# A recurrent attention with a mixture of experts: the first unit's chain of small products reordered, with banks, spare products, gates and weight loads moved

## The chip, the cores and the metric

The kernel runs on one core of a Trainium2 chip. The metric is the device time of one execution in microseconds. TensorE (PE) makes matrix products into PSUM banks, VectorE (DVE), ScalarE (ACT) and GpSimd (POOL) work on tiles, and SyncE (SP) issues nearly all transfers. Each engine takes its own instructions in a fixed order.

## What is computed

For each of 4 x 8 batch and head pairs a 40 x 40 state runs through 768 steps; its outputs, 3072 tokens of 320 values, go through four experts whose outputs are summed with normalised weights. All is float32.

```python
for t in range(S):                      # B=4, H=8, S=768, D=40
    y[:, :, t] = np.einsum('bhd,bhde->bhe', rt, state)
    Sa = np.einsum('bhde,bhe->bhd', state, at)
    state_decay = state * wt[:, :, None, :] - np.einsum('bhd,bhe->bhde', Sa, bt)
    state = state_decay + np.einsum('bhd,bhe->bhde', vt, kt)
...
p = domain_probs / (domain_probs.sum(-1, keepdims=True) + 1e-09)
for e in range(E):                      # E=4, F=1024
    h = np.maximum(x @ w1[e], 0.0)
    out += p[:, e:e + 1] * (h @ w2[e])
```

## The kernel before

The sequence is cut into 12 chunks of 64 steps. A *unit* is one chunk of two batches (16 heads), so there are 24 units; units 0 and 1 are chunk 0. The recurrence inside a chunk becomes products of 64 x 64 matrices and one triangular solve, and only the state passes from chunk to chunk. The mixture takes 128 tokens for units 0 and 1 each and 256 tokens (a whole chunk) from then on; it is most of the work of TensorE.

A unit goes through generators, which a main program written out by hand advances piece by piece with `run(generator, n)`:

- `within(q)` (from L385). Stage 1: the decays are transposed and multiplied up by a scan into G (L398, L402), with `gl` (L400, L406). Stage 2: G is turned on TensorE (pg, L336), and `gp` is made from it with a reciprocal (L414, L415). Stage 3: `n_tok` and `k_tok` (L434, L438), AT (L440, L442). Stage 4: both are turned (pNT, pKT) and copied by ACT to NT and KT (L420). Then come the score products pfe, 32 of which are for F and 32 for ET, into the same two banks (L482 to L488; two instructions of the trace for each product); ACT copies F (L491), DVE copies the upper part to ET (L494). The V and R inputs of units 0 to 2 are turned on TensorE (L450: half plain transposes, half products with the identity that swap halves, one ACT copy each to RT and VT), later units' by DVE. RT and VT make the products pc, masked by DVE into VC (L431). ET and V make pev, copied to EV (L505).
- `substitute(q, eng)` (L513) solves the triangular systems. Four pieces of F are copied to `blocks` (L518: two by ACT, two by DVE), transposed to M (L521), a first pair of columns is taken up (L528 to L537), and 16 pairs of steps fill Z (L544, L554 or L557). DVE does units 0 and 1, GpSimd the others.
- `merge(q)` (L563) transposes Z to Qc and QTc (L568, L570), makes pY and pQ (L583, L595) and puts QT together.
- `step(q)` (L603): psat and pst (L631, L637), copied to SaT and SX; pxr (L651), masked into SX (L660); pdy (L674), from which Y and the new state come (L682 to L693); pxT (L699), copied to xT (L703), the input of the mixture.
- `mixture_of_unit` (L762): for each expert eight blocks of hidden columns in two halves (x0 and x1), `ups` (ph, L726 and L734), and `down` (po, L775), whose result DVE scales and adds to osb (L750, L752). `normalize` (L301) turns the gates (pp, L306) and divides them by their sum on DVE (L307 to L315).

PSUM has two sets of banks: five of the tag `big` for all small products, and three of the tag `mm` for ph and po. The weights of the first layer come in *pieces* of 640 KB (`load_piece`, L263; half an expert), those of the second in 1280 KB for one expert (`load_w2`, L298). The order of instructions on each engine is worked out when the program is built; `keep_in_program_order` (called `pin` in `within`) keeps an instruction where the program has it. `keep_warm(n)` (L931) issues n spare products of the identity (32 and 72 instructions in the trace for n = 16 and 36).

The main program starts at L937: unit 0 goes alone up to its solve on DVE (L950), 36 spare products stand behind pg of unit 1 (L960), then unit 0's merge and step, and from L976 the mixture of unit 0 with units 1 and 2 between. From L1002 a loop over the units does the rest.

Of the kernel before, what the change touches and what calls it, by code (L numbers as in the profile page):

```python
# [7 lines left out]
FP32 = mybir.dt.float32  # L8
# [7 lines left out]
def kernel(  # L16
# [55 lines left out]
    def big(name):  # L72
        return ps.tile([P, 512], FP32, name=name, tag="big", bufs=5)
# [227 lines left out]
    def normalize():  # L301
        n = B // 2 * NC
        pp = big("pp")
        flat = probs.rearrange("p i t e -> p (i t) e")
        for e in range(E):
            nc.tensor.transpose(out=pp[:, e * n:(e + 1) * n], in_=flat[:, :, e], identity=ident[0:n, 0:n])  # L306
        ins = nc.vector.tensor_copy(  # L307
            out=gate[:], in_=pp[:, 0:E * n].rearrange("p (e b c) -> p c b e", b=B // 2, c=NC),
        )
        tc.keep_in_program_order(ins)  # L310
        nc.vector.reduce_sum(out=total[:], in_=gate[:], axis=AX.X)
        nc.vector.tensor_scalar_add(out=total[:], in0=total[:], scalar1=1e-9)
        nc.vector.reciprocal(out=total[:], in_=total[:])
        nc.vector.tensor_mul(gate[:], gate[:], total[:, :, :, None].to_broadcast([P, NC, B // 2, E]))
        nc.vector.tensor_scalar_mul(out=minus_gate[:], in0=gate[:], scalar1=-1.0)  # L315

    def half(s):
# [23 lines left out]
    def tok(x):  # L341
        return lambda j: x[:, 2 * j:2 * j + 2, :].rearrange("p h e -> p (h e)")
# [42 lines left out]
    def within(q):  # L385
# [3 lines left out]
        def pin(ins, also=False):  # L389
            if q.u < PADDED or also:  # L390
                tc.keep_in_program_order(ins)
# [7 lines left out]
        q.gl = sb.tile([P, 2 * NJ, 1], FP32, name="gl", tag="gl", bufs=4)  # L399
        pin(nc.vector.tensor_copy(out=q.gl[:, :, 0], in_=G[:, L::L]))  # L400
        pin(nc.vector.memset(Gv[:, :, 0:1], 0.0))
# [12 lines left out]
        pin(nc.vector.tensor_tensor(out=gp[:], in0=pg, in1=n["W"][:], op=ALU.mult))  # L414
        pin(nc.vector.reciprocal(out=gp[:], in_=gp[:]))  # L415
        yield

# [7 lines left out]

        def causal_scores():
            pc = quadrants(banks("pc"), 0, BY_TOKENS, L, lambda j, s, i: (
                d_half(j, s), i, j, of_slots(VT, d_half(j, s), j, i, D), of_slots(q.RT, d_half(j, s), j, i, D),
            ))
            for r in range(2):  # L430
                pin(causal(of_d_half(q.VC[:, :, D:D + L], r), pc[r]), q.start)  # L431
# [13 lines left out]
        if q.u > 0:  # L445
            nc.scalar.copy(out=q.VC[:, :, 0:D], in_=token_V())
        VT = sb.tile([P, 2 * NJ, L], FP32, name="VT", tag="turned", bufs=3)
        q.RT = sb.tile([P, 2 * NJ, L], FP32, name="RT", tag="RT", bufs=2)

        def turn_padded():  # L450
            for x, t in (("R", q.RT), ("V", VT)):
                p, src = big(f"p{x}T"), n["padded" + x]
                for j in range(NJ):
                    cols = slice(j * P, (j + 1) * P)
                    if j % 2 == 0:
                        nc.tensor.transpose(out=p[:, cols], in_=tok(src)(j), identity=ident[:])
                    else:
                        for s in range(2):
                            nc.tensor.matmul(
                                out=p[half(1 - s), cols], lhsT=src[:, head(j, s), :], rhs=ident[:], start=True, stop=True,  # L460
                            )
                nc.scalar.copy(
                    out=t[:].rearrange("p (i j) t -> p j i t", i=2),
                    in_=p[:].rearrange("p (j i t) -> p j i t", i=2, t=L),
                )

        if q.u >= PADDED:
            turn_raw(VT[:], n["rawV"][:])
            turn_raw(q.RT[:], n["rawR"][:])
        yield  # L470
# [5 lines left out]
        if q.u > 0:  # L476
            if q.u < PADDED:
                turn_padded()
            causal_scores()
            yield  # L480
# [3 lines left out]
            s, i ^ s, j, of_slots(q.AT, s, j, i), of_pairs(NT, s, j, i),  # L484
        ))
        pe = quadrants(p, NJ * L, BY_TOKENS, L, lambda j, s, i: (
            s, i, j, of_pairs(KT, s, j, i), of_slots(q.AT, s, j, i),
        ))  # L488
        q.F = sb.tile([P, H, L], FP32, name="F", tag="F", bufs=2)
        for s in range(2):  # L490
            nc.scalar.copy(out=of_slot(q.F[:], s), in_=pf[s])  # L491
        ET = ETs()
        for s in range(2):
            causal(of_slot(ET[:], s), pe[s])  # L494
        yield
# [12 lines left out]
        if q.u == 0:  # L508
            turn_padded()
            causal_scores()  # L510
        yield

    def substitute(q, eng):  # L513

# [6 lines left out]
        ins = nc.vector.transpose(out=M[:], in_=cols)  # L521
        if q.u == 1 or eng is nc.vector:
            tc.keep_in_program_order(ins)


        pairs = M[:].rearrange("p (c two) r -> p c two r", two=2)
        on_diag = M[:].rearrange("p c r -> p (c r)")[:, Q + 1::2 * (Q + 1)]
        nc.vector.memset(on_diag, 0.0)  # L528

# [3 lines left out]
        below = M[:].rearrange("p c r -> p (c r)")[:, 1::2 * (Q + 1)]  # L533
        nc.vector.tensor_tensor(
            out=by_second, in0=pairs[:, :, 1, :], in1=below[:, :, None].to_broadcast([P, Q // 2, Q]), op=ALU.mult,
        )
        nc.vector.tensor_tensor(out=pairs[:, :, 0, :], in0=pairs[:, :, 0, :], in1=by_second, op=ALU.add)  # L537
        at_once = eng is nc.vector
# [375 lines left out]

    def run(gen, n=99):
        for _ in range(n):
            if next(gen, gen) is gen:
                break
# [17 lines left out]

    ws = [within(units[u]) for u in range(3)]  # L937
    keep_warm(16)
    run(ws[0], 1)
    go(load_raw(units[1], "W"))  # L940
    run(ws[0], 2)
    run(ws[1], 1)
# [6 lines left out]
    run(ws[0], 2)  # L949
    substitute(units[0], nc.vector)  # L950
    run(ws[0], 1)
# [5 lines left out]
    for x in "VR":  # L957
        load_padded(units[2], x)
    run(ws[1], 1)
    keep_warm(36)  # L960
    run(ws[1], 1)
    run(m)
    run(ws[2], 1)
    for e in range(2):
        load_piece()
        load_piece()
        load_w2(e)
    load(units[2], "BK")
    go(load_raw(units[2], "A"))
    go(load_raw(begin(3), "W"))  # L970
    load_piece()
    run(s, 4)
    run(ws[1], 1)
    run(s)
    run(ws[1], 2)
    mixture_of_unit(units[0])  # L976
    substitute(units[1], nc.vector)
    normalize()
    run(ws[1])
# [3 lines left out]
    mix(1)  # L983
    run(ws[2], 2)
    load(units[3], "WBKV")
    go(load_raw(units[3], "AVR"))
    run(m)
    mix(1)
    run(ws[2], 2)
    run(s, 2)  # L990
    run(ws[2], 1)
    substitute(units[2], nc.gpsimd)
    ws.append(within(units[3]))
# [8 lines left out]
    for u in range(1, NU):  # L1002
# [50 lines left out]
        if u + 2 < NU:  # L1053
            substitute(units[u + 2], nc.gpsimd)
        if u + 3 < NU:
            ws.append(within(units[u + 3]))
            run(ws[u + 3], 1)
# [41 lines left out]
```

## Time and profile before

| | |
|---|---|
| median of 7 runs | 1148.47 us (1143.71 to 1153.02) |
| profiled execution | 1147.09 us, of it span 1145.3 us |
| PE busy | 1111.2 us (97%), 16088 products |
| DVE, ACT, POOL busy | 756.7, 335.1, 471.6 us |
| mean granted clock of TensorE | 0.979 |
| transfers | 122.17 MB, mean 107 GB/s |
| ph (L726, L734) | 2280 products, 454.6 us busy |
| products for osb (L841, L775) | 27% and 3% of the chain that ended last |

A row of the timeline has start, duration, engine, line, operation, the tile written and the tiles read, shapes, and a count if several alike are merged; in brackets stand the idle time of the engine before it and what ended it. The chain of waits follows what released each step, back from the last instruction; "issue" in it is time in which an engine waited for nothing that the profile shows. A stretch has the busy time of each engine, then TensorE's granted clock (1.00 is full), the DMA share and GB/s. A busy TensorE can be one at a low clock: its busy time says nothing of its pace.

The mixture's first product starts at 52.58 us and po of expert 0 at 61.27. The solve of unit 0 takes DVE from 22.34 to 32.99 us, that of unit 1 from 60.72 to 71.39. GpSimd starts on unit 2's at 103.34, on unit 3's at 131.64 and on unit 4's at 174.22.

### The profile page before, as it was taken

The numbers are of one execution on the slowest core, as the hardware profiler recorded it, in microseconds if no ns is written. First come the engines' busy times: TensorE is split into PE (matmuls) and PEld (weight loads), VectorE is DVE, ScalarE is ACT, GpSimd is POOL, SyncE is SP. The second block draws the span as 40 slices with busy tenths as digits, with TensorE's granted clock in tenths as the row PEclk, the third lists the DMA queues.
The fourth block names the chain that finished last, engine by engine and source line by source line (L and its number), as shares of the span: only waits on it lengthen the run. The fifth ranks groups of instructions, "written<-read, shape, count | busy, mean of one in ns | idle before, by whom it ended". The sixth has DMA issues, their size and how long they took to land.

```text
span 1145.3 us, 38306 instructions
## 1 busy us (share of the span) xinstructions
PE 1111.2 (97%) x16088; PEld 984.0 (86%) x16088; DVE 756.7 (66%) x1554; ACT 335.1 (29%) x847; POOL 471.6 (41%) x1221
## 2 busy tenths in 40 slices
PE   6899997999999999999999999999999999999998
PEld 5778876888989898888998989989899898888887
DVE  7673657797766867767677677677586686553333
ACT  2222423332342332332332332332322323311110
POOL 4003637644625526526427437346346346340000
PEclk7888999999999999999999999999999999999999
DMA  7874543345353553644543543543444442231320
GB/s 117 235 212 120 107 106 76 91 105 123 79 124 90 125 121 80 139 105 97 129 106 80 143 100 85 134 106 89 117 108 103 117 108 65 76 89 53 104 93 12
DMA packets 268867, 122.17 MB, mean 107 GB/s; under 512 B 213736, under 2 KB 242072, under 8 KB 268696
## 3 DMA queue, kind: packets, MB, share of 16 engines
q1 hardware_dynamic: 265416, 119.12, 42.3%
q8 instruction: 127, 2.08, 0.8%
q10 hardware_dynamic: 3280, 0.61, 0.3%
q14 instruction: 44, 0.36, 0.1%
HBM read 111.79 MB, written 3.93 MB: 101 GB/s over the span
## 4 chain that ended last, share of the span: by engine, by line
PE 85%; DVE 6%; POOL 3%; issue 2%; SPq 1%; DMA 1%; ACT 1%; DVEq 0%; POOLq 0%; ACTq 0%
PE ph L734 29%; PE p L841 27%; PE ph L726 9%; PE pdy L372 3%; PE po L775 3%; POOL Z L557 2%; PE pfe L372 2%; PE psat L372 2%; PE pxr L372 2%; PE prn L372 1%; POOL Z L544 1%; PE pc L372 1%; PE pQ L595 1%; PE pev L372 1%; PE pY L583 1%
## 5 line engine op out<-in xcount | busy, mean ns | idle before, releaser
L734 PE MATMUL ph<-xT,w1p 128*128 128x256 f32 (+1 forms) x1520 | 345.1, 380 | 0.4 <-issue 0.4
L734 PEld LDWEIGHTS ph<-xT,w1p 128*128 128x128 f32 x1520 | 275.2, 191 | 63.2 <-issue 25.3
L544 POOL TENSOR_TENSOR Z<-M,Z 128x62 f32<-128x62 f32 (+7 forms) x352 | 142.2, 404 | 374.8 <-DVE M L537 341.9
L557 POOL TENSOR_TENSOR Z<-Z 128x31 f32<-128x31 f32 (+7 forms) x704 | 256.6, 364 | 55.2
L835 DVE TENSOR_TENSOR a<-hs 128x512 f32<-128x512 f32 x220 | 152.4, 710 | 125.1 <-ACT hs L739 125.1
L739 ACT ACTIVATE hs<-ph 128x512 f32<-128x512 f32 (+1 forms) x208 | 116.0, 564 | 299.5 <-PE ph L734 298.8
L841 PE MATMUL p<-sums,a 128*128 128x160 f32 x1056 | 165.1, 299 | 0.0
L752 DVE SCALAR_TENSOR_TENSOR osb<-p,gate,osb 128x320 f32<-128x320 f32 (+1 forms) x243 | 107.9, 481 | 74.5 <-PE p L841 70.8
L841 PEld LDWEIGHTS p<-sums,a 128*128 128x128 f32 x1056 | 152.9, 190 | 2.3
L726 PE MATMUL ph<-xT,w1p 64*128 64x256 f32 (+1 forms) x760 | 109.5, 399 | 1.8 <-issue 1.7
L841 PE MATMUL p<-w,hs 128*128 128x160 f32 x704 | 102.9, 299 | 0.0
L841 PE MATMUL p<-w,a 128*128 128x160 f32 x704 | 102.8, 299 | 0.0
L841 PEld LDWEIGHTS p<-w,hs 128*128 128x128 f32 x704 | 100.3, 190 | 2.2
L576 POOL COPY QT<-QTc 32x256 f32<-32x256 f32 x96 | 51.4, 535 | 113.5 <-DVE QTc L570 102.9
L841 PEld LDWEIGHTS p<-w,a 128*128 128x128 f32 x704 | 98.0, 190 | 0.0
L726 PEld LDWEIGHTS ph<-xT,w1p 64*128 64x128 f32 x760 | 67.2, 188 | 15.3 <-issue 5.7
L521 DVE STREAM_TRANSPOSE M<-blocks 128x1024 f32<-128x1024 f32 x24 | 47.1, 1962 | 24.9 <-ACT blocks L518 24.1
L415 DVE RECIPROCAL gp<-gp 128x320 f32<-128x320 f32 x24 | 51.7, 2152 | 0.8
L372 PE MATMUL pdy<-SX,n_tok 64*64 64x104 f32 (+1 forms) x768 | 39.7, 249 | 2.8 <-issue 1.4
L372 PE MATMUL pdy<-VC,k_tok 64*64 64x104 f32 (+1 forms) x768 | 41.7, 262 | 0.0
L505 ACT COPY EV<-pev 64x160 f32<-64x160 f32 x96 | 23.4, 286 | 61.5 <-PE pev L372 61.2
L626 ACT COPY SN<-prn 128x256 f32<-128x256 f32 x44 | 15.6, 370 | 84.9 <-DVE RH L621 81.0
(147 smaller groups left out, 1357.8 us busy)
## 6 DMA issues: line engine op xcount, KB each, us to landing
w1p<-in_moe_w_dram SPq DMA_DIRECT2D x95, 512.0 KB
w1p<-in_moe_w_dram SPq DMA_DIRECT2D x190, 64.0 KB
w<-in_moe_w_dram SPq DMA_DIRECT2D x4, 1280.0 KB
sums<-in_moe_w_dram SPq DMA_DIRECT2D x9, 512.0 KB
natW<-in_w_dram SPq DMA_DIRECT2D x48, 80.0 KB
natB<-in_b_dram SPq DMA_DIRECT2D x48, 80.0 KB
natK<-in_k_dram SPq DMA_DIRECT2D x48, 80.0 KB
out_dram<-osb SPq DMA_DIRECT2D x46, 80.0 KB
```

The costliest lines, as they stand in the source:

```text
L372: nc.tensor.matmul(out=p[row][half(col), lo + at * out_cols:lo + (at + 1) * out_cols], lhsT=lhsT, rhs=rhs, start=(n == 0), stop=(n == len( ...
L415: pin(nc.vector.reciprocal(out=gp[:], in_=gp[:]))
L521: ins = nc.vector.transpose(out=M[:], in_=cols)
L544: ins = eng.tensor_tensor(out=Z[:, 1:3, 0:n, j + 1:Q], in0=M[:, j:j + 2, None, j + 1:Q].to_broadcast([P, 2, n, m]), in1=Z[:, here, 0:n, j: ...
L557: eng.tensor_tensor(out=z[:, 0], in0=z[:, 0], in1=z[:, x], op=ALU.add)
L576: ins = nc.gpsimd.tensor_copy(out=q.QT[quarter(i), :, quarter(i % 2)], in_=QTc[quarter(i)])
L726: nc.tensor.matmul(out=ph[i][:, f, :], lhsT=w1.last[i * DT:(i + 1) * DT, f, :], rhs=xT[i * DT:(i + 1) * DT, 2, :], start=(f == 0), stop=False,
L734: nc.tensor.matmul(out=ph[i][:, f, :], lhsT=w1.main[:, g, at * P:(at + 1) * P], rhs=xT[:, g, :], start=False, stop=(g == 1 and f == HF // ...
L739: nc.scalar.activation(out=h[:, i * HF // 2:(i + 1) * HF // 2, 0:n], in_=ph[i][:], func=ACTF.Relu,)
L752: nc.vector.scalar_tensor_tensor(out=to, in0=p, scalar=sc, in1=to, op0=ALU.mult, op1=ALU.add)
L835: nc.vector.tensor_tensor(out=t[:], in0=x, in1=y, op=op)
L841: nc.tensor.matmul(out=p[:, n * HD:(n + 1) * HD], lhsT=a[:, f, :], rhs=b[:, f, :], start=(f == 0), stop=(f == HF - 1),)
```

## The change

In `within`, for unit 0 alone, the products for ET get two banks of their own. ET's copies become a stage of their own behind F's, so that the main program can put the solve's copies and its first operations ahead of them; for units 0 to 2 (and, in DVE's order, 3) they now stand behind M's sum, through the new argument `between` of `substitute` or a `run` after it. The first operations of the solve are all pinned, for all units. V and R of units 0 to 2 are turned by the plain `turn`, and the swap of halves is left to the copies: ACT makes three for each tile, one of 128 and two of 64 partitions. For unit 1 this happens ahead of its reciprocal's products, before unit 0's pY. `gl` is taken by a product with `first` (which is one there) and not by a copy. `normalize` becomes a generator: its products and an ACT copy come early, its divisions on DVE behind unit 2's scan. In the main program 10 spare products stand behind the first pg, 18 in the place of 36 before pY; pNT and pKT of unit 1 come before pxr of unit 0; the stages of unit 2 are advanced in other places; the first two pieces are loaded ahead of natB, natK, rawA and rawW, and both second-layer weights and the next pieces behind these.

```diff
@@ normalize
-        ins = nc.vector.tensor_copy(
-            out=gate[:], in_=pp[:, 0:E * n].rearrange("p (e b c) -> p c b e", b=B // 2, c=NC),
-        )
-        tc.keep_in_program_order(ins)
-        nc.vector.reduce_sum(out=total[:], in_=gate[:], axis=AX.X)
+        nc.scalar.copy(out=gate[:], in_=pp[:, 0:E * n].rearrange("p (e b c) -> p c b e", b=B // 2, c=NC))
+        yield
+        tc.keep_in_program_order(nc.vector.reduce_sum(out=total[:], in_=gate[:], axis=AX.X))
...
+        yield
@@ within
-            if q.u < PADDED or also:
+            if q.u <= PADDED or also:
...
-        pin(nc.vector.tensor_copy(out=q.gl[:, :, 0], in_=G[:, L::L]))
+        pin(nc.vector.tensor_tensor(out=q.gl[:], in0=G[:, L::L][:, :, None], in1=first[:, :, 0:1], op=ALU.mult))
...
+        def turn_rv():
+            VT = sb.tile([P, 2 * NJ, L], FP32, name="VT", tag="turned", bufs=3)
+            q.RT = sb.tile([P, 2 * NJ, L], FP32, name="RT", tag="RT", bufs=2)
+            for x, t in (("V", VT), ("R", q.RT)):
+                if q.u >= PADDED:
+                    turn_raw(t[:], n["raw" + x][:])
+                    continue
+                p = turn(f"p{x}T", tok(n["padded" + x]), q.u == 1)[:].rearrange("p (j i t) -> p j i t", i=2, t=L)
+                to = t[:].rearrange("p (i j) t -> p j i t", i=2)
+                nc.scalar.copy(out=to[:, 0::2], in_=p[:, 0::2])
+                for r in range(2):
+                    nc.scalar.copy(out=to[half(r), 1::2], in_=p[half(1 - r), 1::2])
+            return VT
+
+        if q.u == 1:
+            VT = turn_rv()
         yield
...
+        if q.u == 0:
+            p = banks("pe")
         pe = quadrants(p, NJ * L, BY_TOKENS, L, lambda j, s, i: (
...
             nc.scalar.copy(out=of_slot(q.F[:], s), in_=pf[s])
+        yield
+
         ET = ETs()
         for s in range(2):
-            causal(of_slot(ET[:], s), pe[s])
+            pin(causal(of_slot(ET[:], s), pe[s]), q.start)
         yield
@@ substitute
-    def substitute(q, eng):
+    def substitute(q, eng, between=None):
...
+        run(between)
         at_once = eng is nc.vector
@@ main program
+    norm = normalize()
     keep_warm(16)
     run(ws[0], 1)
     go(load_raw(units[1], "W"))
-    run(ws[0], 2)
+    run(ws[0], 1)
+    keep_warm(10)
+    run(ws[0], 1)
...
-    substitute(units[0], nc.vector)
+    substitute(units[0], nc.vector, scores_of_first())
...
+    load_piece()
+    load_piece()
     run(ws[1], 1)
-    keep_warm(36)
+    run(norm, 1)
+    keep_warm(18)
     run(ws[1], 1)
     run(m)
     run(ws[2], 1)
-    for e in range(2):
-        load_piece()
-        load_piece()
-        load_w2(e)
+    run(norm)
     load(units[2], "BK")
     go(load_raw(units[2], "A"))
     go(load_raw(begin(3), "W"))
+    load_w2(0)
     load_piece()
-    run(s, 4)
+    load_piece()
+    load_w2(1)
+    load_piece()
+    run(s, 2)
     run(ws[1], 1)
     run(s)
     run(ws[1], 2)
     mixture_of_unit(units[0])
-    substitute(units[1], nc.vector)
-    normalize()
+    substitute(units[1], nc.vector, scores_of_second())
     run(ws[1])
     mix(3)
     m, s = merge(units[1]), begin_step(1)
     run(m, 1)
     mix(1)
-    run(ws[2], 2)
+    run(ws[2], 1)
+    run(m)
+    run(s, 2)
+    run(ws[2], 1)
     load(units[3], "WBKV")
     go(load_raw(units[3], "AVR"))
-    run(m)
     mix(1)
-    run(ws[2], 2)
-    run(s, 2)
+    run(ws[2], 3)
+    substitute(units[2], nc.gpsimd)
     run(ws[2], 1)
-    substitute(units[2], nc.gpsimd)
...
             substitute(units[u + 2], nc.gpsimd)
+        run(w, 1)
```

## What was predicted

> **What bounds the kernel now.** I read the page first, then the chain of waits up to 175 us, the timeline of every engine up to 130 us, and the table of 2 and 10 us stretches with their granted clock. The page's slices:
>
> ```profile
> PE   6899997999999999999999999999999999999998
> PEclk7888999999999999999999999999999999999999
> ```
>
> From the third slice on TensorE is full nearly everywhere, and the second row shows a lowered clock only in the first four. 300 to 1000 us holds 3.2 us of idle PE, and the change leaves TensorE's order there as it is. So there are two places to gain: the chain of the first unit before the mixture starts, and idle or slow-clock time up to about 200 us. The timeline of the first 36 us:
>
> ```profile
> 12.59 1.08 PE L336 MATMUL pNT<-ident,n_tok 128*128 128x128 f32 x4 [3.57 <-DVE n_tok L434]
> 14.85 1.23 DVE L402 TENSOR_TENSOR_SCAN G<-G,first 128x512 f32<-128x512 f32 x1
> 16.50 0.65 ACT L491 COPY F<-pfe 128x256 f32<-128x256 f32 x2 [1.35 <-PE pfe L372]
> 16.97 0.77 DVE L383 COPY_PREDICATED ET<-mask_up,pfe 128x256 f32<-128x256 int32 x2 [0.69 <-ACT F L491]
> 17.64 0.81 ACT L518 COPY blocks<-F 32x256 f32<-32x256 f32 x2
> 18.49 1.93 DVE L521 STREAM_TRANSPOSE M<-blocks 128x1024 f32<-128x1024 f32 x1 [0.27 <-ACT blocks L518]
> 26.86 9.00 PE L934 MATMUL warm<-ident 128*128 128x128 f32 x72
> ```
>
> F waits 1.35 us for score products that share its banks; the blocks stand behind ET on DVE and behind a V copy on ACT; and pY, at 35.79, starts only when the 72 spare instructions end, although QTc was there at 34.15. The chain of waits then has:
>
> ```profile
> 44.32 1.43 issue
> 45.74 1.13 PE pdy L372 x17
> 46.87 1.04 PE pNT L336 x4
> 47.92 0.85 PE pKT L336 x4
> 48.77 1.51 PE pxT L699 x12
> ...
> 77.39 2.16 DVE gp L415
> 79.58 0.50 DVE n_tok L434
> 80.13 1.11 PE pNT L336 x4
> 81.24 0.85 PE pKT L336 x4
> ...
> 90.93 3.17 PE ph L734 x16
> 94.10 0.65 PE ph L726 x8
> 94.75 1.98 PE ph L734 x16
> ```
>
> Sixteen ph instructions take 3.17 us at 90.93 and 1.98 at 94.75: after TensorE waited for unit 2's n_tok, it ran to 93.4 at half clock, as the stretch shows (columns: us, PE, PEld, DVE, ACT, POOL, clock, DMA share, GB/s):
>
> ```profile
> 80.00:90.00 10.00, 9.19 (x130) 6.69 (x132) 4.07 (x11) 3.43 (x8) 0.00 (x0) 0.50 0.57 99
> ```
>
> **First unit to QTc.** Ten spare products are 20 instructions; full clock passes 11 per us, half clock 6 (the warm row cut by 1 us). They fill 9.0 to 10.9 and leave 1.6 idle instead of 3.57. [...] by it pNT to pe run at full clock (0.44 us for four turns as at 118 us, not 1.08), so that with own banks F starts at 14.5, at half clock 15.6, not 16.5. But DVE's row decides: its scan for unit 1 and gl end at 16.28 whatever TensorE does, then its blocks take 0.57. So M starts at 16.9, 1.6 earlier[...]. ET (0.77) now stands between M's sum and Z: the first Z step comes at 21.5 instead of 22.34, QTc 0.85 us earlier. The gl copy as a product (0.25 or 0.17 us against 0.17 of the gl row after it) is worth at most 0.1: nothing.
>
> **TensorE's filling up to pY.** In the changed order it holds pev, V and R turns of unit 0, pc, pg, V and R turns of unit 1, pp and 36 spare instructions. ET ends at 21.1, so at half clock pev ends 22.3 and EV's copies 23.3. Each turn is now four plain transposes (0.9) instead of 2.06 us of mixed products, but three ACT copies (F and RS rows: some 1.0) instead of one of 0.58: VT 24.3, RT 25.4, pc 26.2, pg 27.1, V turn of unit 1 28.0. The built program gives R's turn the same bank, so it waits for V's three copies (29.1), and pp for R's (31.3). Spare products: 32.0 on, 20 slow and 16 fast, to 36.9. pY: 37.0, 1.2 late. Bounds: 33.7, where Qc, QTc and the first VC copy free it, and 38. I take 37.0, since transposes alone did not raise the clock at 80 to 86 us.
>
> **To the end of pe of unit 1.** pY to pxr took 6.0 us; pNT and pKT of unit 1 now stand before pxr (0.9 to 1.9, middle 1.3, part of it hidden by the SaT copies), and pxr's bank also waits for two SX copies. SX: 44.0, not 42.21. DVE would be ready at 42.7: 42.29, less 0.85, plus 1.34 for the five gate operations moved in (71.58 to 72.92), less 0.1. So these are covered by 1.3 us; without that cover they cost 1.3. The gate copy on ACT lies in a wait. pdy took 4.66 us from SX, 1.43 of it "issue". [...] the row costs 1.43 at 351 GB/s of transfers, and three of the nine such stops of the run come after the 475th, 2268th and 12123rd product[...]. [...] the same count falls into pdy again, but the queue is empty from about 33 to 37 now, since natB of unit 2 waits for n_tok with both w2 behind it. I take 0, with 1.4 in the range. pdy ends at 47.0 (46.87 before). Then 8.15 us to the end of pe (55.02) become 3.8: Y 0.8, pxT 1.34, pc 0.6, pfe and pe 1.0. Out go pNT and pKT (1.9) and the turns (2.4). End of pe: 50.8, 4.2 earlier.
>
> **New waits, to the end of po of expert 1.** This took 21.35 us (to 76.37). ET of unit 1 now comes behind M (pe end +5.15 to 5.95), and queued behind pev are two ph rows and po: TensorE has 4.5 us of work, waits 1.1. Second, the built program puts the second half of expert 1's ph into the bank of po 0, which DVE frees (L750) late in unit 1's Z steps: pe end +16.6, against +14.0 for TensorE: 2.6. That wait costs all po and pg behind it. Less pp (0.6) and a split ph row (0.6), this stretch takes 23.6. End of po 1: 74.4, 2.0 earlier.
>
> **Unit 2.** From there to pY of unit 2 at 125.92 it was 49.55 us. Now pY, pQ, psat and eight ph rows of x0 and x1 stand ahead of pNT, so n_tok (ready 4 us on) is covered; this returns the half clock (5.7: pNT 1.08, turns 1.45, pc 0.5, psat 0.6, ph 1.7, pQ 0.38) and 1.6 of turns. The waits of 0.46, 1.16, 0.69, 0.95 give way to others: pQ 0.35, psat 0.2, pc 1.0 (six ACT copies), pev 1.1, pY 0.3, where POOL's 19.9 us of Z bind. Two po rows (1.1) move behind. Sum: 8.7, at 40.9 us. Those rows and 0.5 of ph come before unit 4's pc, and from its pe to its pY 31.35 us pass on DVE and POOL whatever TensorE does (4.53 of waiting):
>
> ```profile
> 198.30 1.07 PE L583 MATMUL pY<-QTc,F 32*32 32x32 f32 x32 [4.53 <-DVE QTc L570]
> ```
>
> so 1.6 is given back. ET behind M for unit 3 costs 0: po (4.3) hides it.
>
> [...] 76.2 to 79.6 lost the clock with waits of 0.46 and 1.16 only (1.7 for 3.4 us of half clock); I take half, 0.8.
>
> **Sum.** 2.0 + 8.7 - 1.6 - 0.8 = 8.3. The profiled execution took 1147.09 (span 1145.3 and 1.8 around it), so 1138.8; the median of the runs lies 1.4 above that execution: 1140.
>
> **Weights moved back.** natB, natK, rawA and rawW go first; w2 of expert 0 starts near 41.5, when the scan for unit 2 has released rawW. Two w2 (1.31 MB each) and two pieces (0.66) follow: at the 260 GB/s of 60 to 70 us they have landed at 57; po 0 needs the first at 58 (there at 46.5), po 1 the second at 70. Cost 0.
>
> **Rivals.** (1) The waits only move: [...] the clock falls wholly at the 2.6 wait (0.9 more) and again at the pev wait of unit 2 (1.7): gain 4.3, 1144. For it: half clock in the first 50 us. (2) More of the gain stays: spare products end before QTc (2.4) and po 0 gets out of Z's way (2.6 and 0.8): gain 14, 1134.5. For it: 33.7 is possible when the clock rises at 28. Against: the bank is fixed in the program. (3) Slower: the second w2 is late. At 137 GB/s it lands just at 70; every us later is a us lost at po 1. At 106 (78.4) the gain is gone, at 90 (85) it is about 1155. For it: 93 to 127 GB/s at 46 to 56 us; against: those were input rows in small packets, while weights ran at 250 to 350.
>
> **How the numbers follow.** My sum, 1137 to 1142.5: 0.50. Rival 2, with what lies between: 0.22. Rival 1, 1142.7 to 1147: 0.24. Rival 3: 0.04. 0.5% (5.7 us, about what a measurement of this kernel tells from no change) ends at 1142.7, so faster 0.72, same 0.24, slower 0.04. The range 1132 to 1146 leaves the ends of the rivals out.
>
> **What will show it.** M of unit 0 near 16.9 and ET after its sum; pY near 37; no "issue" in pdy; a wait of TensorE for osb L750 in expert 1's second ph; clock 1.0 from there to pY of unit 2, near 115; a wait of about 6 us at unit 4's pY. I am wrong if those waits are absent or twice as long, or if a w1p, sums or w2 transfer releases TensorE.

## The result, and the profile after

The changed kernel takes 1145.24 us (median of 22 runs, 1140.5 to 1150.76) beside 1150.32 us of the kernel before on the same chips (57 runs). The ratio is 0.9957, with a 95% interval of 0.9942 to 0.9971. So it is faster by 4.9 us, 3.3 to 6.7, where 8.3 had been forecast: the direction was right, the size was not.

The profiled execution takes 1145.7 us (span 1143.7), only 1.6 us less in span than the one of before. The slices of its page:

```profile
PE   6899998999999999999999999999999999999998
PEclk8899997999999999999999999999999999999999
```

The row of the clock has changed: it is higher in the first, third and fourth slice, and lower in the seventh (171 to 200 us). The first unit, in the timeline of every engine:

```profile
12.45 0.63 PE L335 MATMUL pNT<-ident,n_tok 128*128 128x128 f32 x4 [1.21 <-DVE n_tok L450]
14.50 0.65 ACT L488 COPY F<-pfe 128x256 f32<-128x256 f32 x2 [0.31 <-PE pfe L371]
16.74 1.90 DVE L519 STREAM_TRANSPOSE M<-blocks 128x1024 f32<-128x1024 f32 x1
20.17 0.76 DVE L382 COPY_PREDICATED ET<-mask_up,pe 128x256 f32<-128x256 int32 x2
32.47 7.02 PE L936 MATMUL warm<-ident 128*128 128x128 f32 x36
39.42 0.69 PE L583 MATMUL pY<-QTc,F 32*32 32x32 f32 x32
```

F waits 0.31 us and not 1.35, and M starts 1.75 us earlier. But 36 spare instructions take 7.02 us, where 72 took 9.00, and pY starts at 39.42, 3.6 us later than before, though QTc was there at 33.05. The chain of waits then has the two places that cost most:

```profile
67.82 0.47 DVE osb L750
68.29 0.04 issue
68.33 0.81 PE ph L726 x8
69.14 3.54 PE ph L734 x16
...
131.56 1.63 issue
```
```profile
68.33 0.81 PE L726 MATMUL ph<-xT,sums 64*128 64x128 f32 x8 [1.88 <-DVE osb L750]
```

TensorE waited 1.88 us for the first osb, as its own timeline says, and the sixteen ph instructions behind it took 3.54 us, nearly all of it at a clock of 0.50 (69.0 to 72.4 us), where 1.98 is full clock. At 131.56 it stood for 1.63 us with nothing that the profile shows to wait for. Unit 2's stretch, on the other hand, is now at full clock. The stretches of the two kernels (us, PE, PEld, DVE, ACT, POOL, clock, DMA share, GB/s), first before, then after:

```profile
0.00:40.00 40.00, 28.88 (x378) 25.07 (x382) 33.42 (x81) 8.45 (x20) 14.33 (x51) 0.77 0.78 161
80.00:130.00 50.00, 47.79 (x744) 39.48 (x745) 24.83 (x50) 15.25 (x41) 18.15 (x53) 0.87 0.44 100
```
```profile
0.00:40.00 40.00, 27.77 (x284) 25.39 (x284) 34.05 (x85) 10.24 (x26) 14.57 (x51) 0.74 0.67 124
80.00:130.00 50.00, 47.86 (x887) 39.87 (x889) 29.65 (x59) 19.57 (x56) 23.56 (x65) 1.00 0.59 134
```

The lead of the changed kernel over the one before, at the same piece of work in these two executions:

| | lead forecast, us | lead in the profile, us |
|---|---|---|
| pY of unit 0 | -1.2 | -3.6 |
| end of pdy of unit 0 | -0.1 | -1.1 |
| end of pe of unit 1 | 4.2 | 2.95 |
| end of po of expert 1 | 2.0 | -0.6 |
| pY of unit 2 | 10.7 | 6.6 |
| pY of unit 3 | | 3.3 |
| pY of unit 4 | | 3.5 |
| osb at 313 us | 9.1 less 0.8 | 3.8 |
| end | 8.3 | 1.6 |

**One pair of profiles is not the difference of two kernels.** A second profile of each (`before_again` and `again` below) gives other leads: 2.7 us at pY of unit 2, -1.2 at 313 us and -1.6 at the end, for the same two programs. What differs from execution to execution is the clock (13.7 and 3.4 us at half around unit 2 in the kernel before) and the length of the stops (0.54 and 3.03 us in the first ph of the changed one). Therefore the runs are compared by two numbers below: the ratio of the times, and the mean granted clock over all runs. The clock record of the traces holds the values 1.00 and 0.50, so 2 x (1 - mean clock) x span is the time at half clock: 48 us in the first profile of before, 41 in that of the changed kernel.

| kernel | median us (runs) | ratio to before, 95% | mean clock | at half clock, us |
|---|---|---|---|---|
| before | 1151.05 (96) | | 0.9786 | 49 |
| changed | 1145.24 (22) | 0.9957 (0.9942 to 0.9971) | 0.9835 | 38 |
| po_big | 1140.85 (6) | 0.9930 (0.9912 to 0.9948) | 0.9852 | 34 |
| spread | 1145.10 (12) | 0.9956 (0.9939 to 0.9973) | 0.9848 | 35 |
| spare6 | 1148.42 (22) | 0.9991 (0.9979 to 1.0003) | 0.9796 | 47 |
| shift12 | 1148.78 (14) | 0.9982 (0.9959 to 1.0005) | 0.9835 | 38 |
| both | 1139.27 (6) | 0.9906 (0.9881 to 0.9930) | 0.9863 | 31 |
| both0 | 1143.15 (6) | 0.9918 (0.9886 to 0.9949) | 0.9838 | 37 |
| both0_gates | 1140.77 (7) | 0.9909 (0.9878 to 0.9940) | 0.9831 | 38 |
| b_u2 | 1150.22 (20) | 0.9993 (0.9974 to 1.0012) | 0.9791 | 48 |
| no10 | 1148.34 (22) | 0.9956 (0.9938 to 0.9974) | 0.9797 | 47 |

(The row of before holds the runs that stood beside the experiments, on three chips whose medians are 1149.9, 1151.8 and 1152.2; each ratio is to the runs on its own chip. Two slow runs of b_u2, over 1.5% above its quickest, are left out. Since the chips differ, ratios are compared below, not medians.)

The 96 runs of the kernel before show what half clock costs: those with a mean clock of 0.976 took 1155.0 us on average (9 runs), those with 0.979 1150.5 (27), those with 0.981 1148.9 (8). That is 6.1 us for 11.5 us at half clock (0.005 x 2 x 1150), one half, as for work that is TensorE's throughout. It holds from run to run of one kernel; between kernels it is rough, as the table shows: no10 has the ratio of the changed kernel with 9 us more at half clock, and shift12 has its clock and not its ratio.

### The profile page after: what moved, and what is told of

Read it like the earlier page. It is cut to its first block, busy times and chain, and to the rows that moved or that the text cites. A ratio compares the mean times of both kernels' runs of the same rounds, so it can differ in the third digit from the quotient of the medians.

```text
span 1143.7 us, 38245 instructions
## 1 busy us (share of the span) xinstructions
PE 1106.3 (97%) x16036; PEld 981.9 (86%) x16036; DVE 756.7 (66%) x1553; ACT 338.3 (30%) x860; POOL 475.7 (42%) x1221
## 4 chain that ended last, share of the span: by engine, by line
PE 88%; DVE 5%; POOL 2%; ACT 2%; DMA 1%; issue 1%; SPq 1%; DVEq 0%; ACTq 0%
PE ph L734 30%; PE p L841 28%; PE ph L726 9%; PE pdy L371 4%; PE po L775 2%; PE pfe L371 2%; PE psat L371 2%; PE pxr L371 2%; PE prn L371 2%; PE pc L371 1%; PE pQ L595 1%; PE pY L583 1%; PE pev L371 1%; POOL Z L557 1%; PE pg L335 1%
## 5 line engine op out<-in xcount | busy, mean ns | idle before, releaser
L734 PE MATMUL ph<-xT,w1p 128*128 128x256 f32 (+1 forms) x1520 | 344.9, 380 | 1.7 <-issue 1.6
L734 PEld LDWEIGHTS ph<-xT,w1p 128*128 128x128 f32 x1520 | 274.7, 191 | 65.4 <-issue 27.1
L739 ACT ACTIVATE hs<-ph 128x512 f32<-128x512 f32 (+1 forms) x208 | 115.8, 564 | 298.0 <-PE ph L734 297.5
L600 ACT COPY QT<-pQ 32x256 f32<-32x256 f32 x48 | 17.4, 363 | 79.0 <-PE pQ L595 78.5
```

The costliest lines, as they stand in the source:

```text
L734: nc.tensor.matmul(out=ph[i][:, f, :], lhsT=w1.main[:, g, at * P:(at + 1) * P], rhs=xT[:, g, :], start=False, stop=(g == 1 and f == HF // ...
L739: nc.scalar.activation(out=h[:, i * HF // 2:(i + 1) * HF // 2, 0:n], in_=ph[i][:], func=ACTF.Relu,)
```

## The experiments

Theory A: the gain is smaller than forecast because TensorE stays at half clock up to 38 us and falls to it again behind the wait for osb. Rival B: stops of TensorE have moved to other places of the program and cost more there. Rival C: GpSimd's solves swallow what TensorE gains in the first 80 us.

**again**: the changed kernel without an edit.

> The changed kernel itself, a second profile. Theory A (stops that the profile puts down to issue fall where they like): the stops of over 1 us that the first profile has at 131.6, 414.3 and 721.4 us are at other products or absent, while waits for another engine, the half clock from 18 to 38 us and the one behind the wait for osb return at the same places; pY of unit 2 at 119.3 within 0.5; the span differs by up to 4 us from 1143.7. Theory B (they belong to fixed places of the program): all three return at the same products with over 1 us, and the span is within 1 us.

The waits ahead of pY and the half clock of the start came again (16.9 to 37.4 us). The wait for osb did not: a stop of 3.03 us in ph (0.54 in the first profile) had made TensorE so late that osb was there before it, and half clock came behind that stop instead, from 54.4 to 61.3:

```profile
55.21 0.80 PE L726 MATMUL ph<-xT,w1p 64*128 64x128 f32 x3 [3.03 <-issue]
```

The other stops came again at the same products: 1.91 us at 132.7, 1.02 at 416, 2.37 at 723. So theory A of this run is wrong on the stops and B right on their places, not on the time: the lengths change, and the span was 1147.3, 3.6 us longer. pY of unit 2 came at 120.5.

**before_again**: the kernel before without an edit.

> The kernel before, a second profile. Theory B (stops without a releaser belong to fixed places of the instruction stream; the second profile of the changed kernel and the two kernels with its count of products had them at the 598th, 1736th, 6040th and 10721st product again): the stops return at the 476th, 2269th, 7441st, 10100th and 12124th product, each between 0.3 and 2.5 us, and the stretch from 316 us to the end is 828.7 us within 1.5. Theory A (they fall anywhere): at most one of them returns.

Five of five places return (1.28, 0.44, 2.91, 1.04 and 0.52 us). But the stretch from 314 us to the end took 831.7 us, not 828.7; the two profiles of the changed kernel have 830.9 and 832.1. So in these four profiles the steady part shows no difference between the two kernels that stands clear of the change from run to run. The stretch of unit 2 is a surprise:

```profile
80.00:90.00 10.00, 8.20 (x142) 6.18 (x143) 5.54 (x12) 4.83 (x12) 0.00 (x0) 0.83 0.62 116
```

In the first profile its clock was 0.50 and half clock lasted from 79.7 to 93.4; here it lasted 3.4 us. In return this execution was at half clock from 39.9 to 50.1.

**shift12**: 12 more spare instructions in a rest of 5.8 us, nothing else moved.

```diff
     run(ws[0], 2)
+    keep_warm(6)
     def scores_of_first():
```

> The changed kernel with 6 more spare products (12 instructions) in the 5.8 us in which TensorE waits for the first ET; nothing else moves. Theory B with places set by the count of instructions [...]: the stops at psat of 416 and 723 us are gone or shorter than 0.5 us and others stand elsewhere, since every later product is 12 further on; the stretch from 313 us to the end changes from 831 by up to 3 us, towards the 828.7 of the kernel before. Theory B' (places set by the transfers of that moment): psat at 416 and 723 us waits again with over 1 us, the stretch stays at 831 to 832. On the clock: half from 17.8 or 21.2 us, to 38.3 in both, so pY at 39.4 as now.

The stops at psat near 416 and 723 are gone, others came at 551.7 (2.17 us) and 861.6 (2.08); the stretch to the end did not shrink (832.3 us), and the ratio, 0.9982, is clear neither of the changed kernel's nor of 1. pY came at 38.5 and half clock ended at 36.5, where 39.4 and 38.3 had been expected. The two early ones remain at the same count, and so stand at other work, 12 products earlier in the program. Here the stop that had been in ph at 131.56 in the changed kernel, in TensorE's timeline:

```profile
131.02 0.68 PE L371 MATMUL pxr<-RT,SN 64*64 64x64 f32 x30
134.59 0.21 PE L371 MATMUL pxr<-RT,SN 64*64 64x64 f32 x1 [2.90 <-issue]
134.73 0.71 PE L726 MATMUL ph<-xT,w1p 64*128 64x128 f32 x8
```

It broke off pxr between the last two of its products. Counted in products from the start of the trace (a few records are missing), the stops without a releaser, with their length, are these (left out are those that stay with one piece of work, wherever the count puts it: 0.55 us at unit 0's psat, 0.33 in ph near 260 us, 0.5 to 0.75 in ph near 371; those at 8065 and 13377 the profile puts down to a transfer of rawV):

```
before          476 (1.43)   2269 (0.44)   7441 (0.73)   10100 (1.05)   12124 (0.42)
before_again    476 (1.28)   2269 (0.44)   5417 (0.53)   7441 (2.91)   10100 (1.04)   12124 (0.52)
changed         598 (0.54)   1736 (1.63)   6040 (1.51)   10721 (2.10)
again           598 (3.03)   1736 (1.91)   6040 (1.02)   8063 (0.37)   10721 (2.37)   12743 (1.45)
shift12         598 (1.52)   1736 (2.90)   8065 (2.17)   12743 (2.08)
no10            598 (0.30)   4017 (1.47)   8696 (1.29)   13377 (2.41)
both0           4017 (1.50)  8696 (1.55)   13377 (2.02)
```

The distances are multiples of about 126.5: 10721 - 6040 and 13377 - 8696 are 37 of them, 12743 - 10721 is 16, 1736 - 598 is 9. That makes some 126 such places in 16036 products; at three to six of them in a row TensorE stops, for 0.3 to 3 us each, and together that comes to 4 to 10 us.

The page of the changed kernel has a DMA queue whose packets fit this step (packets, MB, share of the DMA engines):

```profile
q8 instruction: 126, 2.06, 0.7%
```

That is 16 KB a packet, and one packet for 127 products (16036 / 126). In the trace's record of packets every stop of the table ends 1.25 to 1.83 us after one of them landed (1.43, 1.32, 1.55 and 1.45 us in the changed kernel), and 9 packets lie between the stops at 598 and 1736, 37 between those at 6040 and 10721, as the steps have it. The exception is the 2269th product, whose last packet had landed 4.6 us or more before: it is none of these places. I read these stops as waits of TensorE for its own instructions; the counts and the landings fit that, but the profile names no releaser, so it is not shown.

Where such a stop is long, the traces show one of two things. The packet of the stop at 598 started 3.2 us after the product one step before it in the changed kernel (50.55 and 47.35 us), at a DMA share of 1.07 between the two, and 5.7 us after it in again, at a share over 1 too; in spread and both, which have no stop there, it started 1.2 and 0.8 us after, at shares of 0.65 and 0.64. And ahead of the stop at 10721 in the changed kernel TensorE went through the step before, all of it short products, in 2.2 us (719.2 to 721.4). That the count fixes the places is what again and shift12 show; that full DMA engines or short products make a stop long is read from these traces, and was not tried by itself.

**no10**: the ten spare products behind the first pg taken out.

```diff
     run(ws[0], 1)
-    keep_warm(10)
     run(ws[0], 1)
```

> The changed kernel without the ten spare products behind the first pg; the stream is 20 instructions shorter. My step (DVE's scan and gl of unit 1 set M; the clock adds nothing there): the clock falls at about 11.4 us, F comes 0.5 to 1.1 later, M at 16.9 to 17.3 instead of 16.7, pY within 0.5 of 39.4. Theory B: the stop at the 1736th product, 1.6 to 2.9 us long in six kernels, is gone, since that place in the stream now lies 20 products later, among ph; pY of unit 3 then comes 1.5 to 2 us earlier than in the changed kernel (164.7), and the median is at or below its ratio of 0.9957. Rival (the ten products are worth their time): median 1 us or more above it.

M starts at 16.68 and pY at 38.9, as with them: they bring nothing to the chain. The stop at the 1736th product is gone. TensorE's timeline, where the changed kernel stood for 1.63 us behind the third ph of L734:

```profile
129.77 0.71 PE L726 MATMUL ph<-xT,w1p 64*128 64x128 f32 x8
130.42 1.83 PE L734 MATMUL ph<-xT,w1p 128*128 128x128 f32 x14
```

pY of unit 3 comes at 162.4 instead of 164.7. The ratio is the changed kernel's, with 9 us more at half clock: if the clock lost about 4 us, the stop gave back a part of it, and the rest lies within the intervals; that split is not shown.

**spare6**: 6 in the place of 18 ahead of pY.

```diff
-    keep_warm(18)
+    keep_warm(6)
```

> The changed kernel with 6 instead of 18 spare products ahead of pY of unit 0. Theory A (the clock decides[...]): pY starts near 34.9 instead of 39.4, but at half clock, which lasts until the mixture's products: SX near 42.6 instead of 45.5, pe of unit 1 ends near 52 as now, and 1.7 us or more are lost in the first ph: median 0 to 2 us above the changed kernel's 1145.2. Theory D (spare products cost what they last): everything from pY on comes 4 us earlier, pe of unit 1 ends near 48, median near 1142.

pY came at 35.25, SX at 44.1 and pe of unit 1 ended at 50.7 (theory A had 42.6 and 52); half clock lasted to 44.6 us. Its profile is the quickest of its executions (1142.8); by the ratios it is 3.9 us slower than the changed kernel, with 9 us more at half clock. Theory A held in direction, D (spare products cost what they last) fell: here they are worth more than they last.

**spread**: the 18 spare products dealt out, to see when the clock rises (at 38.2 us in the changed kernel).

```diff
                 for r in range(2):
                     nc.scalar.copy(out=to[half(r), 1::2], in_=p[half(1 - r), 1::2])
+                if q.u == 1:
+                    keep_warm(4)
...
-    keep_warm(18)
+    keep_warm(10)
```

> The changed kernel with its 18 spare products ahead of pY dealt out: 4 behind V's turn and 4 behind R's turn of unit 1, in waits for ACT's copies that last 1.2 us each, and 10 behind pp. Theory A [...]: it rises near 34.9 or before instead of 38.3, pY starts at 34.5 to 36 instead of 39.4, SX comes near 42.5 (DVE's divisions of the gates end at 42.4 and bind then), pe of unit 1 ends near 49.2 instead of 52.1: 1.5 to 3 us are left at the end, median near 1143. Theory C (GpSimd's solves swallow it): pe of unit 1 early, pY of unit 4 as now, median within 0.7 of 1145.2.

In TensorE's timeline:

```profile
28.08 1.91 PE L938 MATMUL warm<-ident 128*128 128x128 f32 x8
29.79 1.06 PE L335 MATMUL pRT<-ident,padded 128*128 128x128 f32 x4
30.64 1.27 PE L938 MATMUL warm<-ident 128*128 128x128 f32 x8
32.65 2.50 PE L938 MATMUL warm<-ident 128*128 128x128 f32 x20
35.08 0.69 PE L585 MATMUL pY<-QTc,F 32*32 32x32 f32 x32
```

Eight spare instructions take 1.91 us, the next eight 1.27: the clock rose at 31.1, after 3.4 us without rest, and twenty then take 2.50. pY started at 35.1, SX at 42.5, po of expert 1 ended 3.6 us earlier, all as theory A had it. Yet the ratio did not move. The wait for osb has grown to 2.85 us (DVE's solve is no faster), and pY of unit 4 came only 2.3 us earlier, then at half clock for 10.2 us instead of 6.8. So the step was right for the chain and worth nothing alone.

**po_big**: the first po in a bank of the other set.

```diff
-            po = ps.tile([P, DM], FP32, name="po", tag="mm", bufs=3)
+            own = q.u == 0 and e == 0
+            po = big("po")[:, 0:DM] if own else ps.tile([P, DM], FP32, name="po", tag="mm", bufs=3)
```

> The changed kernel with po of expert 0 of unit 0 in a bank of the other set, so that the second half of expert 1's ph does not wait for DVE's first osb. Theory A (that wait and what it does to the clock are a good part of what is missing): the wait of 1.9 us and the half clock at 69.0 to 72.4 (1.7) are gone; po of expert 1 ends near 73.4 instead of 77.0, pY of unit 2 near 115.8 instead of 119.3, and 1.5 to 3.5 us of it last to the end: median near 1142.5 where the changed kernel has 1145.2. Theory C (GpSimd's solves swallow what TensorE gains in the first 80 us): po of expert 1 early as well, but pY of unit 4 at 194.8 as now, median within 0.7 of the changed kernel's.

The ph behind po 0 run through, while DVE takes po 0 up at 67.84, when it likes:

```profile
66.49 0.71 PE L726 MATMUL ph<-xT,sums 64*128 64x128 f32 x8
67.13 2.05 PE L734 MATMUL ph<-xT,sums 128*128 128x128 f32 x16
69.02 4.47 PE L776 MATMUL po<-w,hs 128*128 128x320 f32 x16
```

po of expert 1 ends at 73.5 and pY of unit 2 starts at 115.8, as expected to 0.1. The ratio falls by 0.0027, about 3.1 us (the intervals overlap by 0.0006), most of the wait and its half clock. pY of unit 4 was at 194.3 in this profile, as rival C has it, but for another reason: a stop of 2.62 us at 130.8 and half clock behind it had taken the lead. The next kernel decides on C.

**both**: spread and po_big together.

> Own bank for po of expert 0 and the spare products dealt out, together. Theory A (both are on the path and TensorE's lead is handed on): pY of unit 0 at 35.1, po of expert 1 ends near 70.5, pY of unit 2 near 113, pY of unit 4 near 190 with its wait still near 4.4 us, since that is 31 us of DVE and GpSimd behind its score products; median 1138 to 1140. Theory C (a lead before unit 2 is swallowed): pY of unit 4 at 193 or later, median 1141 or more, as with the bank alone.

po of expert 1 ended at 70.8, pY of unit 2 started at 113.2 and of unit 4 at 188.3, 6.5 us earlier than in the changed kernel. Rival C falls: the solves hand the lead on. Ratio 0.9906, outside the interval of the changed kernel; the least half clock of all (31 us). This version beats both kernels; to the kernel before it is 10.8 us (0.0094 of 1150).

**both0** and **both0_gates**: both without the last ten spare products, and then the gate operations of DVE moved behind unit 0's state.

```diff
-    keep_warm(10)
...
     run(m)
     run(ws[2], 1)
-    run(norm)
...
     run(s)
+    run(norm)
     run(ws[1], 2)
```

> Own bank for po of expert 0, 4 and 4 spare products in the waits for ACT, and none behind pp: 20 instructions fewer in the stream than the changed kernel. Theory B (the stops without a releaser stand at every 126.5th product of the stream, where it so happens that few products of the mixture lie just ahead): the boundaries at the 598th and 1736th product now fall 20 products later, among long ph products, and their stops (0.5 and 1.2 to 2.9 us) are gone, those at psat near 410 and 717 us too; others may come at new products. pY of unit 0 at 33.3 to 33.6, SX at 42.5 all the same, since DVE's gate operations end then; pY of unit 2 near 112.5, median 1136 to 1138.5. Rival (stops are as frequent elsewhere, and what is gained ahead of SX is nothing): median 1139 to 1141, as both.

> As both0, and the five gate operations of DVE stand behind unit 0's new state instead of ahead of SX. My step said that they lie under a cover of 1.3 us; with pY 4 us earlier that cover is gone. If so SX comes at 41.2 to 41.8 instead of 42.5, and pe of unit 1 and all behind it 0.7 to 1.3 us earlier, up to 1 us at the end. Rival (pxr is not there sooner, since psat to pxr run at half clock): SX moves by less than 0.4, the end by nothing.

The stops at 598 and 1736 are gone as expected. But in both0 TensorE waited 2.03 us in pdy for SX, which stood behind DVE's gate operations, and the clock was at half from 44.0 to 50.8 behind it:

```profile
42.98 0.30 PE L371 MATMUL pdy<-SX,n_tok 64*64 64x104 f32 x1 [2.03 <-DVE SX L382]
```

There is 6 us more of half clock than in both. The ratio of both0, 1140.6 on a kernel before of 1150, is not the 1136 to 1138.5 of theory B, and neither ratio can be told from that of both: the rival (stops as frequent elsewhere, nothing gained ahead of SX) is nearer. SX, in DVE's timeline of both0 and of both0_gates:

```profile
42.37 0.21 DVE L313 TENSOR_SCALAR minus_gate<-gate 128x96 f32<-128x96 f32 x1
42.49 0.77 DVE L382 COPY_PREDICATED SX<-mask_up,pxr 128x256 f32<-128x256 int32 x2
```
```profile
41.50 0.77 DVE L382 COPY_PREDICATED SX<-mask_up,pxr 128x256 f32<-128x256 int32 x2 [0.34 <-PE pxr L371]
```

With pY early DVE's gate operations do bind, and moving them brings SX 1.0 us forward. The wait in pdy is gone with them, and in the profile pe of unit 1 ends at 48.05 and not at 51.72; in the ratios (0.9909 and 0.9918) this cannot be told. In the changed kernel, where pxr is ready at 45.4, they are hidden.

**shared**: unit 0's ET products in F's banks again.

```diff
-        if q.u == 0:
-            p = banks("pe")
```

> The changed kernel with unit 0's ET products in the banks of its F products again. My step (DVE's scan and gl of unit 1 set the start of M): F's copies end 0.45 us later, M starts at 16.7 to 16.9 as now, and nothing later moves by more than 0.2. Rival (the banks bring the gain in M): F waits over 0.8 us, M starts at 17.3 or later and everything up to Z is as much later.

F waited 0.80 us, M started at 17.09, which is 3.22 us after the first pfe, not 2.99. So the banks are worth 0.2 us here: between the two, nearer to my step.

**b_u2**: the kernel before with the order around unit 2's stages alone: unit 1's psat and pst ahead of unit 2's pNT, the load of unit 3 behind it.

```diff
-    run(ws[2], 2)
-    load(units[3], "WBKV")
-    go(load_raw(units[3], "AVR"))
+    run(ws[2], 1)
     run(m)
+    run(s, 2)
+    run(ws[2], 1)
+    load(units[3], "WBKV")
+    go(load_raw(units[3], "AVR"))
     mix(1)
-    run(ws[2], 2)
-    run(s, 2)
-    run(ws[2], 1)
+    run(ws[2], 3)
```

> The kernel before with one part of the change: unit 1's psat and pst and the load of unit 3 in the order that the change has for unit 2, so that psat and pst stand ahead of unit 2's pNT (the ph rows do not come ahead of it here). My step (unit 2's stretch held TensorE at half clock, 5.7 of 8.7 us): the 1.2 us wait for n_tok goes, the clock stays up, and from po of expert 1 to pY of unit 2 it takes 42 to 43.5 us instead of 48.9; median ratio to the kernel before 0.994 to 0.997. Rival E (that half clock of 13.7 us was one execution's; the second profile has 3.4): the stretch takes 43.5 to 45, the ratio is 0.998 to 1.001.

Its profile has unit 2's stretch at full clock and 43.2 us from the end of the second osb (that of po of expert 1) to pY, as my step said; it is the quickest of its 22 executions, 7 us below the next. The median says what the change is worth: nothing that shows (0.9974 to 1.0012, where my step had 0.994 to 0.997), with 48 us at half clock. The ph rows ahead of pNT, which the changed kernel has besides, were not tried alone.

## Why the prediction was wrong in size

- **M at 16.9, Z at 21.5, QTc 0.85 earlier**: right (16.74, 21.23, 1.1). That DVE bounds M and the ten spare products add nothing to it: right (no10, shared). That they would keep the clock up to pe was no more than an estimate; it fell at 17.8 us and not at 11.5, and pNT took 0.63 us instead of 1.08.
- **pY at 37.0**: wrong by 2.4 us, and above the bound of 38. The failed step is "20 slow and 16 fast": I let the clock rise within 3.4 us of the first spare product. It rose at 38.2, with 0.5 us of rest from 31.4 to 34.8 and none from there on, and the 36 instructions took 7.02 us where 4.9 had been taken; waits of 1.2 us for ACT's copies stood ahead of it. spread filled them, and pY came at 35.1.
- **SX at 44.0, pdy at 47.0, pe of unit 1 at 50.8**: each 1.0 to 1.5 late after a pY 2.4 late. The cover of the gate operations was right (DVE ready at 42.44, said 42.7), its price without cover too (1.0, said 1.3). The stop in pdy went, as I had estimated. From the product one step before to the start of the packet the DMA share was 0.73 (42.9 to 43.9 us) where it had been 1.04 (39.1 to 43.3); so the reason, an emptier queue, fits, though two profiles do not show it, but not its time, which is not the quiet from 33 to 37. I had not asked where the next such place falls. It fell into the first ph, 0.54 to 3.03 us. And three stops were too few to read the places from: the step is 126.5 products, and one of the three, behind the 2268th, is none of them.
- **The wait for osb**: named rightly, 1.88 us instead of 2.6 since TensorE came later, and absent in the second profile, where it came later still. Its risk for the clock, booked at half (0.8), which was an estimate, came whole in the first: 1.7 us for 3.4 at half clock (69.0 to 72.4). With it po of expert 1 ended at 77.0 and not at 74.4. po_big puts the whole term at about 3.1 us, near the 3.4 booked.
- **Unit 2, 8.7 us**: this is the term that misled most. From the end of po of expert 1 to pY the change gained 7.2 us in the first pair of profiles and 3.5 in the second; "this returns the half clock (5.7)" took the luck of one execution for a property of the kernel: the second profile of the kernel before has 3.4 us of half clock there, not 13.7, and from the second osb to pY it took 45.2 us and not 48.9. b_u2, one part of this step, brings that stretch down in its profile and nothing in its ratio; the ph rows were not tried.
- **1.6 given back at unit 4**: right in place and size. The lead fell from 4.8 us to 3.3 at pc of unit 4, and from its pe to its pY 31.1 us passed (31.35 said). The wait there was 2.64 us in the profile and 4.86 in the second, not 6, because half clock and a stop had come before it.
- **The stops without a releaser** were put at nothing, but for pdy. The one at the 1736th product took 1.2 to 2.9 us in seven profiles of kernels with this count up to there. The change has 52 products fewer and so moved every such place: three profiles with the old count (the kernel before twice, b_u2) have 3.1 to 6.3 us of such stops, six with the new one (the changed kernel twice, po_big, spread, both, shared) 3.9 to 10.2, on average 4.3 and 6.5. About 2 us may have been lost so; nine profiles that differ this much do not show it.
- **Weights at no cost**: right; no transfer of w2 releases TensorE.
- Of the rivals, the first (the waits only move, 1144) came nearest, though not by its own sum: of its three losses (1.4 us for a stop in pdy again, 0.9 and 1.7 for the clock) the stop came in another place and the clock fell behind the wait for osb, but it stayed up at the pev wait of unit 2 (1.00 from 80 to 130 us). The 11 us less at half clock would be 5.6 us of time if TensorE needs all of it, and the measured gain is 4.9, so the clock alone could make the gain. That it does is not shown: no10 keeps the ratio with 47 us at half clock. How the missing 3.4 us divide between unit 2, the late pY and the stops stays open; only the profiles tell the place, and two of one kernel differ by more.

## What to carry to other kernels

Before a gain is sized from a stretch at half clock or from a stop without a releaser, look at a second execution: all nine stops of the first profiles of the two kernels stood at the same counts of products in the second, but lengths and half clocks change from run to run, and with them the time, by 13 us among the 96 runs of the kernel before, while this whole change is worth 5. And 12 or 20 instructions early in the program moved later stops to other work here (shift12, no10), and a gain of 1 to 3 us can belong to that. With spare products in the short waits between other products the clock rose sooner here than with a block of them behind (31.1 and 38.2 us). Where a product waits for a bank that a late engine frees, another bank for that one product can take the wait away, as in po_big (1.88 us in the changed kernel).

## What the runs showed of the hardware

In the clock record of the first two profiles each time at 0.50 lasted 3.4 us or a multiple of it: 11.5 to 28.5, 38.8 to 42.2, 45.6 to 49.0, 79.7 to 93.4 and 195.8 to 206.0 us in the kernel before; 17.8 to 38.2, 69.0 to 72.4, 171.4 to 178.2, 195.3 to 202.1 and 724.3 to 727.7 in the changed one. In the last 3.4 us before these ten rises TensorE rested (ran no product) for 0.15 us at most. But it had none from 171.4 to 174.8 and from 195.3 to 198.7 either, among short products, and the clock stayed at 0.50. In the last 3.4 us before the ten falls it rested for 1.2 to 2.9 us. But the stop of 1.63 us at 131.56 in the changed kernel was not followed by 0.50, and in spread the clock stayed up behind the wait of 2.85 us for osb. What decides between them was not tried by itself.

The queue that the page calls instruction brought 126 packets of 16 KB in the changed kernel, one for 127 products of TensorE, and the stops at steps of 126.5 products ended 1.25 to 1.83 us after the landing of one of them.
